# Input checks next to their operands' first readers, and the gate checked through the output's row sums

## The chip, the cores and the metric

The kernel runs on one core of a Trainium2 chip. The time is the device time of one execution in microseconds (us); less is better. The engines of the core are named as the profile names them: PE (TensorE, the matmuls; PEld its weight loads), DVE (VectorE), ACT (ScalarE), POOL (GpSimd) and SP, whose queue issues the DMAs. Each engine works through its own list of instructions in order, and they wait for each other by semaphores.

## The reference

Three blocks follow each other on 4 batches of 768 tokens with 8 heads of 48 (384 features):

```python
for t in range(S):                                   # gated linear attention, state 48x48 for each head
    state = alpha[:, :, t, :, None] * state + einsum('bhd,bhe->bhde', k[:, :, t], v[:, :, t])
    y[:, :, t] = einsum('bhd,bhde->bhe', q[:, :, t], state)
xn = (x - mean) / sqrt(var + 1e-6) * g_ln            # first MLP, x is y with the heads side by side
x = x + maximum(xn @ w_ch1, 0) @ w_ch2               # 384 -> 1536 -> 384
h = gelu(x @ w_in)                                   # second MLP: 384 -> 1024 = u (512) and v (512)
v_n = (v - mean) / sqrt(var + 1e-6) * g_ln2
v_s = einsum('ts,bsd->btd', w_sg, v_n) + b_sg        # mixes all 768 tokens of a batch
out = x + (u * v_s) @ w_out                          # 512 -> 384
```

All inputs and the output are float32. The mixing by `w_sg` needs v_n of a whole batch, so the gate and the output of a batch follow its last chunk.

## The kernel before

**Two halves for each number.** The fast path multiplies in float16: each factor is split into a high half (a copy to float16) and a low half (the rest), and three products (high by high, high by low, low by high) are added in PSUM. The copies to the high half run on ACT, the low halves mostly on DVE or POOL (the helper `low`, L155). This is sound only while the numbers keep within certain windows, so the kernel gathers statistics as it goes: `accum_out` of an instruction writes a sum for each partition into a column of a small table (st_in, st_g, st_xs and others). At the end of the program a chain of small DVE instructions (L1107 to L1114) compares the tables with their bounds and yields one flag. With the flag set a slow float32 path would compute everything anew; in the runs here it stays unset.

**Chunks and units.** 24 chunks of 128 tokens (6 for each batch) pass through attention (`att_steps`), two chunks form a group for the MLP work, and the MLP work is cut into units:

- A (L717): hidden layer of the first MLP, one PSUM tile pg at a time from a ring "g" of three; ACT takes the high half with the ReLU (hT, L722) and DVE the low half (hT, L723). The next A matmuls need a free PSUM tile, and B needs hT.
- B (L752): second matrix of that MLP; DVE adds the residual (L755, with a row sum).
- T: splits x (L151, L152) and transposes it by DMA, and squares x on ACT (L775).
- C (pgv L799, pgu L828): first matrix of the second MLP; ACT applies the GELU (vg L802, uT L831), DVE normalizes v.
- D (pgs L856): the mixing by `w_sg`, once a batch; DVE adds the bias (tm, L862), POOL multiplies by u (L865), ACT copies the high half (L869), the low half follows, and ACT squares the gate tm into a scratch tile for the sum st_g (L872). This last trio is held back in `gate_pending` and issued in order behind later work.
- E (pgo L890): the output product; DVE adds the residual (x, L892), and SP writes the result.

**Attention of a chunk from 6 on.** Decays come as scans over alpha (F and K; L361 from chunk 8 on). For chunks from 8 on q, k and alpha are transposed through a copy on ACT (L298), a DMA transpose on SP (L301) and a joining copy on ACT (L314). F is scaled by q and K by k (L319, `scaled`), F is copied to qs (L446), K to kh (L468), kh is transposed by DMA to ks, K is rescaled on ACT (L482), the scores sc (L490) are masked on DVE (L503) and split into ss (L522 on ACT, low half on DVE). v is split into vs (L549 on ACT, L551 on DVE). The state's update psd (L585) needs vs and ks, the output psy (L621) needs ss and vs. The state is split into sp (L647), y is normalized (L654 to L661) into xsp and goes by DMA to xhT, which A reads.

**The input checks** stand in a step of their own behind the split of v (`stats`): ACT squares q, k and v (L564, three instructions a chunk), DVE takes the largest alpha (L567). The squares' results go to a scratch tile from a ring "cv" of two buffers (`junk`), which the gate squares (L872), the squares of x (L775) and the pieces of w_sg on their way to the DMA transposes (wsp, L221) use too. A buffer of that ring comes free when its last use is done. The raw inputs of a chunk lie in one of two buffers (inp); the next chunk but one is loaded into it by four DMAs on SP when all its readers are done.

**What sets the order.** Every step and unit gets a planned time, all are sorted by it, and the program is written in that order. The framework's scheduler then builds each engine's list from its own estimate of when an instruction can run, so an instruction that is made free earlier can move past others on every engine. `issue_after` and `in_order` hold an instruction behind a named one.

## Time and profile before

| | us |
|---|---|
| median of 3 runs (lowest to highest) | 686.86 (686.51 to 688.11) |
| profiled execution, its own time | 688.59 |
| its span | 686.8 |
| PE busy | 640.7 |
| DVE busy | 442.2 |
| ACT busy | 412.1 |
| POOL busy | 237.3 |

The span is the traced part of the profiled execution; 1.79 us of its own time lie outside. The mean granted TensorE clock of the span is 0.981 of full speed. "L717 PE MATMUL pg<-xhT,w1s" in a row is the kernel's line, the engine, the operation, and the tiles written and read; "[1.67 <-DVE hT L723]" behind a stretch says that the engine stood idle for 1.67 us before it and that DVE's hT of line 723 ended that.

### The profile page before, as it was taken

To read this page: it belongs to the slowest core of one execution; us is meant where nothing else is said; L and a number is where in the kernel's file an instruction comes from. 1 tells how busy PE (TensorE), PEld (TensorE's weight loads), DVE (VectorE), ACT (ScalarE), POOL (GpSimd) and SP (SyncE) were. 2 spreads that over 40 slices of the span, in tenths; PEclk is the share of its full clock that TensorE was granted. 3 is DMA by queue.
4 is the path that set the end of the run, shared out by engine and by line. 5 is a ranking of instruction groups with operands and counts; after the bars stand their busy time and mean duration, and the time that the engine had idled before them with its cause. 6 is when DMAs were issued, how large, how long until landed. Compare 5 with 4: busy or idle time off the path is not lost.

```text
span 686.8 us, 14367 instructions
## 1 busy us (share of the span) xinstructions
PE 640.7 (93%) x5622; PEld 487.2 (71%) x5622; DVE 442.2 (64%) x852; ACT 412.1 (60%) x787; POOL 237.3 (35%) x462
## 2 busy tenths in 40 slices
PE   5989798989999989999999989998989999999995
PEld 3677586667676876677677876676666986676783
DVE  6799977867745576557745569658756686233334
ACT  3765445687873698498773788767663873232230
POOL 4132210533423650443533751532405660301251
PEclk9999979999999998999999999999999999999999
DMA  9996879648363468466263387754263402200102
GB/s 226 279 246 177 259 168 185 105 88 118 64 107 53 72 110 152 105 113 110 48 112 51 60 116 158 123 105 70 51 89 62 86 17 70 24 12 12 35 2 75
DMA packets 228637, 70.64 MB, mean 103 GB/s; under 512 B 219472, under 2 KB 222544, under 8 KB 228560
## 3 DMA queue, kind: packets, MB, share of 16 engines
q1 hardware_dynamic: 228560, 69.63, 53.3%
q8 instruction: 46, 0.75, 0.5%
q14 instruction: 31, 0.25, 0.1%
HBM read 35.79 MB, written 4.72 MB: 59 GB/s over the span
## 4 chain that ended last, share of the span: by engine, by line
PE 51%; DMA 15%; DVE 14%; ACT 11%; issue 4%; POOL 2%; SPq 1%; ACTq 0%; DVEq 0%; POOLq 0%
PE pg L752 12%; PE pg L717 10%; PE pgs L856 9%; PE pgo L890 5%; PE pgu L828 5%; DMA stage<-stage 5%; PE pgv L799 4%; DMA wgs<-wsp 3%; ACT stage L314 2%; DMA stage<-in_moe_w_ch_dram 2%; DMA xhT<-xsp 2%; DMA inp<-in_q_dram 2%; ACT stage L298 2%; PE sc L490 1%; DVE sc L503 1%
## 5 line engine op out<-in xcount | busy, mean ns | idle before, releaser
L717 PE MATMUL pg<-xhT,w1s 128*128 128x256 f16 (+1 forms) x1404 | 152.5, 268 | 10.6 <-DVE hT L723 9.4
L717 PEld LDWEIGHTS <-w1s 128*128 128x128 f16 x1404 | 130.1, 100 | 28.7 <-issue 9.0
L752 PE MATMUL pg<-w2s,hT 128*128 128x384 f16 x864 | 146.6, 328 | 0.4 <-DVE hT L723 0.4
L752 PEld LDWEIGHTS <-hT 128*128 128x128 f16 x864 | 83.8, 98 | 54.3 <-issue 1.4
L856 PE MATMUL pgs<-wgs,vn 128*128 128x256 f16 x864 | 96.0, 273 | 0.0
L856 PEld LDWEIGHTS <-vn 128*128 128x128 f16 x864 | 84.1, 98 | 10.3
L723 DVE SCALAR_TENSOR_TENSOR hT<-pg,hT 128x512 f16<-128x512 f32 (+1 forms) x74 | 49.2, 673 | 44.8 <-ACT hT L722 44.6
L314 ACT ACTIVATE stage<-stage 128x1024 uint16<-128x1024 uint16 x48 | 64.4, 1351 | 16.2 <-DMA stage<-stage 16.2
L298 ACT ACTIVATE stage<-inp 128x1024 uint16<-128x1024 uint16 x48 | 49.8, 1051 | 26.2 <-DVE K L361 8.8
L155 POOL TENSOR_TENSOR kh<-K,kh 128x512 f16<-128x512 f32 x17 | 21.0, 1238 | 102.3 <-ACT kh L468 102.3
L722 ACT ACTIVATE hT<-pg 128x512 f16<-128x512 f32 (+1 forms) x74 | 42.0, 572 | 17.5 <-PE pg L717 17.1
L828 PE MATMUL pgu<-x2T,wis 128*128 128x256 f16 x432 | 49.6, 273 | 1.7 <-ACT vg L802 0.9
L799 PE MATMUL pgv<-wis,x2T 128*128 128x512 f16 x216 | 49.3, 379 | 1.8 <-DVE hT L723 1.8
L890 PE MATMUL pgo<-wos,uT 128*128 128x384 f16 x288 | 48.6, 326 | 0.1
L828 PEld LDWEIGHTS <-wis 128*128 128x128 f16 x432 | 41.8, 98 | 8.3 <-issue 1.8
L155 POOL TENSOR_TENSOR qs<-F,qs 128x512 f16<-128x512 f32 x18 | 20.2, 1121 | 76.8 <-ACT qs L446 76.8
L865 POOL TENSOR_TENSOR tm<-tm,uT 128x512 f32<-128x512 f32 x24 | 32.9, 1372 | 23.6 <-DVE tm L862 23.2
L890 PEld LDWEIGHTS <-uT 128*128 128x128 f16 x288 | 27.7, 98 | 18.0 <-issue 0.3
L862 DVE SCALAR_TENSOR_TENSOR tm<-pgs,g2c,bbc 128x256 f32<-128x256 f32 x48 | 20.9, 477 | 28.9 <-PE pgs L856 17.6
L799 PEld LDWEIGHTS <-x2T 128*128 128x128 f16 x216 | 20.5, 97 | 24.0 <-issue 1.9
L522 ACT ACTIVATE ss<-sc 128x512 f16<-128x512 f32 x36 | 20.8, 591 | 24.0 <-DVE sc L503 23.9
L869 ACT ACTIVATE uT<-tm 128x512 f16<-128x512 f32 x24 | 15.0, 626 | 30.0 <-POOL tm L865 30.0
(184 smaller groups left out, 1094.0 us busy)
## 6 DMA issues: line engine op xcount, KB each, us to landing
stage<-in_moe_w_ch_dram SPq DMA_DIRECT2D x24, 384.0 KB, 5.3
inp<-in_alpha_dram SPq DMA_DIRECT2D x24, 192.0 KB, 3.6
inp<-in_q_dram SPq DMA_DIRECT2D x24, 192.0 KB, 3.4
inp<-in_k_dram SPq DMA_DIRECT2D x24, 192.0 KB, 4.0
inp<-in_v_dram SPq DMA_DIRECT2D x24, 192.0 KB, 4.3
out_dram<-x SPq DMA_DIRECT2D x24, 192.0 KB, 1.9
stage<-in_moe_w_in_dram SPq DMA_DIRECT2D x4, 768.0 KB, 4.8
stage<-in_moe_w_sg_dram SPq DMA_DIRECT2D x6, 384.0 KB, 4.1
```

Of the source, the lines that this page charges most:

```text
L155: (nc.vector if on_dve else nc.gpsimd).tensor_tensor(out=out, in0=in0, in1=in1, op=ALU.subtract)
L298: nc.scalar.activation(out=sp, in_=t[:, n].rearrange("p h d -> p (h d)").bitcast(U16) .rearrange("p (x w) -> p w x", w=2), func=AF.Copy)
L314: nc.scalar.activation(out=words[:, :, :, gap:], in_=tr, func=AF.Copy)
L717: nc.tensor.matmul(out=pg[:, f, :], lhsT=w1s[:, a, kk, ff * P:(ff + 1) * P], rhs=xhT[j][:, r, kk, o], start=(n_ == 0), stop=(n_ == 3 * KD ...
L722: nc.scalar.activation(out=hi, in_=src, func=AF.Relu)
L723: last_dve[0] = nc.vector.scalar_tensor_tensor(out=lo, in0=src, scalar=0.0, in1=hi, op0=ALU.max, op1=ALU.subtract)
L752: nc.tensor.matmul(out=box[s], lhsT=hidden(a, f, s), rhs=w2s[:, r, f, :], start=(f == 0 and a == 0 and r == 0), stop=(f == KF - 1 and r == 1))
L799: nc.tensor.matmul(out=pg, lhsT=x2T[j][:, a, kk, o], rhs=wis[:, r, kk, DG:DI], start=(n_ == 0), stop=(n_ == 3 * KD - 1))
L828: nc.tensor.matmul(out=pg[:, f, :], lhsT=wis[:, a, kk, ff * P:(ff + 1) * P], rhs=x2T[j][:, r, kk, 0:N], start=(n_ == 0), stop=(n_ == 3 * K ...
L856: nc.tensor.matmul(out=pg[:, f, :], lhsT=vn[b * NCH + s][:, a, d * P:(d + 1) * P], rhs=wgs[th][:, r, s, :], start=(n_ == 0), stop=(n_ == 3 ...
L865: nc.gpsimd.tensor_tensor(out=tm, in0=tm, in1=uT[key][:, o, :], op=ALU.mult)
L890: nc.tensor.matmul(out=pg, lhsT=gt[key][:, d // 2, a, d % 2, o], rhs=wos[:, r, d, :], start=(d == 0 and a == 0 and r == 0), stop=(d == KG ...
```

## The change

For the 18 chunks from 6 on, the squares of q and k leave the step behind the split of v. They are issued in the step that takes the low half of kh and starts the transpose to ks, each held behind the first instruction that reads the scaled operand (the copy to qs, the copy to kh). The largest alpha is issued in the same step, held behind the scaling of F. The square of v stays where all three were. In the gate, L872 stays for the last batch only (six of 24), and st_g shrinks to six columns. For batches 0 to 2 the output's residual addition gets an `accum_out`, which writes the row sum of each of the 18 output chunks to a new table st_o; the flag's chain compares it with its bounds in three more DVE instructions.

```diff
-    st_g = big.tile([P, NC], F32, name="st_g")
+    st_g = big.tile([P, 6], F32, name="st_g")
+    st_o = big.tile([P, NC - NCH], F32, name="st_o")
...
-                scaled("F", "q")
+                T["q scaled"] = scaled("F", "q")
...
-                nc.scalar.activation(out=T["qs"][:, 0], in_=T["F"], func=AF.Copy)
+                T["q read"] = nc.scalar.activation(out=T["qs"][:, 0], in_=T["F"], func=AF.Copy)
...
                 low(chosen(HB), T["kh"][:, 1], T["K"], T["kh"][:, 0])
                 if "ks" not in T:
                     work(["ks"], F16)
+
+                for n, first in enumerate((T["q read"], T["k read"][0])):
+                    with tc.issue_after(first.ins):
+                        square(n)
+                with tc.issue_after(T["q scaled"].ins):
+                    nc.vector.tensor_reduce(out=st_in[:, i, 3:4], in_=t[:, 3, :, 0:D], op=ALU.max, axis=AX.XY,
+                                            apply_absolute_value=True)
                 nc.sync.dma_start_transpose(out=T["ks"].rearrange("p a n d -> p (a n) d"),
                                             in_=T["kh"].rearrange("p a n t -> p (a n t)"))
...
+        def square(n):
+            nc.scalar.activation(out=junk()[:, 0:DM].rearrange("p (h d) -> p h d", h=H), in_=t[:, n, :, 0:D],
+                                 func=AF.Square, accum_out=st_in[:, i, n:n + 1])
...
         def stats():
             with tc.issue_after(T["v last"][0].ins):
-                for n in range(3):
-                    nc.scalar.activation(out=junk()[:, 0:DM].rearrange("p (h d) -> p h d", h=H),
-                                         in_=t[:, n, :, 0:D], func=AF.Square, accum_out=st_in[:, i, n:n + 1])
-            with tc.issue_after(T["v last"][1].ins):
-                nc.vector.tensor_reduce(out=st_in[:, i, 3:4], in_=t[:, 3, :, 0:D], op=ALU.max, axis=AX.XY,
-                                        apply_absolute_value=True)
+                square(2)
...
-                        n_ = b * 6 + 2 * th + dp
-                        nc.scalar.activation(out=junk()[:, 0:512].rearrange("p (a b) -> p a b", a=2), in_=tm,
-                                             func=AF.Square, accum_out=st_g[:, n_:n_ + 1])
+                        if b == B - 1:
+                            n_ = 2 * th + dp
+                            nc.scalar.activation(out=junk()[:, 0:512].rearrange("p (a b) -> p a b", a=2), in_=tm,
+                                                 func=AF.Square, accum_out=st_g[:, n_:n_ + 1])
...
                 nc.vector.scalar_tensor_tensor(out=xs[i], in0=pg, scalar=1.0 / (S_G * S_WO), in1=xs[i],
-                                               op0=ALU.mult, op1=ALU.add)
+                                               op0=ALU.mult, op1=ALU.add,
+                                               accum_out=st_o[:, i:i + 1] if b < B - 1 else None)
...
-            (st_g, 0.0, 2.0 ** 31, [NC]),
+            (st_g, 0.0, 2.0 ** 31, [6]),
+            (st_o, -1e30, 1e30, [NC - NCH]),
```

The diff shows little of what moves, since the scheduler sets the lists. Three places follow; in the changed kernel the same instruction has a line number one to twelve higher (L314 is L315, L722 is L729, L522 is L534, the squares are L494, x's square L782).

**ACT, between the gate of batch 0 and its output product.** xsp is the split of an attention output or of x, uT<-tm the high half of the gate, hT the hidden layer's high half, inp_94 and inp_95 (inp_95 and inp_96 in the changed kernel) the two input buffers. Before:

```order
L446 ACTIVATE qs<-F 128x512
L314 ACTIVATE stage<-stage 128x2x512
L647 ACTIVATE sp<-state 128x384
L549 ACTIVATE vs<-inp_95 128x384
L314 ACTIVATE stage<-stage 128x2x512
L660 ACTIVATE xsp<-psy,nmu 128x384
L151 ACTIVATE xsp<-x 128x384
L722 ACTIVATE hT<-pg 128x512
L869 ACTIVATE uT<-tm 128x512
L872 ACTIVATE junk,st_g<-tm 128x512
L775 ACTIVATE junk,st_xm<-x 128x384
L722 ACTIVATE hT<-pg 128x512 x2
```

Now:

```order
L447 ACTIVATE qs<-F 128x512
L494 ACTIVATE junk,st_in<-inp_96 128x384 x2
L654 ACTIVATE sp<-state 128x384
L315 ACTIVATE stage<-stage 128x2x512
L561 ACTIVATE vs<-inp_96 128x384
L667 ACTIVATE xsp<-psy,nmu 128x384
L152 ACTIVATE xsp<-x 128x384
L494 ACTIVATE junk,st_in<-inp_96 128x384
L729 ACTIVATE hT<-pg 128x512
L876 ACTIVATE uT<-tm 128x512
L729 ACTIVATE hT<-pg 128x512 x2
```

The three input squares now stand ahead of the first hT (two of them ahead of sp and vs); the gate square and x's squares no longer stand between the first hT and the next two. A gate square just ahead of qs, above the rows shown, is gone as well. The same holds one batch later.

**DVE at the same place.** Before:

```order
L551 SCALAR_TENSOR_TENSOR vs<-inp_95,vs 128x384
L567 TENSOR_REDUCE st_in<-inp_95 128x1
L661 SCALAR_TENSOR_TENSOR xsp<-psy,st_mv,xsp 128x384
L152 SCALAR_TENSOR_TENSOR xsp<-x,xsp 128x384
L723 SCALAR_TENSOR_TENSOR hT<-pg,hT 128x512
L155 TENSOR_TENSOR uT<-tm,uT 128x512
L503 TENSOR_TENSOR sc<-sc,causal 128x512 x2
L361 SCALAR_TENSOR_TENSOR F<-stage,reset 128x516
L361 SCALAR_TENSOR_TENSOR K<-stage,reset 128x516
L723 SCALAR_TENSOR_TENSOR hT<-pg,hT 128x512 x2
```

Now:

```order
L563 SCALAR_TENSOR_TENSOR vs<-inp_96,vs 128x384
L668 SCALAR_TENSOR_TENSOR xsp<-psy,st_mv,xsp 128x384
L153 SCALAR_TENSOR_TENSOR xsp<-x,xsp 128x384
L730 SCALAR_TENSOR_TENSOR hT<-pg,hT 128x512
L156 TENSOR_TENSOR uT<-tm,uT 128x512
L730 SCALAR_TENSOR_TENSOR hT<-pg,hT 128x512
L515 TENSOR_TENSOR sc<-sc,causal 128x512
L730 SCALAR_TENSOR_TENSOR hT<-pg,hT 128x512
L515 TENSOR_TENSOR sc<-sc,causal 128x512
L362 SCALAR_TENSOR_TENSOR F<-stage,reset 128x516
L362 SCALAR_TENSOR_TENSOR K<-stage,reset 128x516
```

The second and third hT moved from behind both score masks and both scans to ahead of the scans, and the reduction of alpha left this place.

**ACT while the last weights are prepared** (chunk 6; wsp are the pieces of w_sg). Before:

```order
L151 ACTIVATE wsp<-stage 128x768
L722 ACTIVATE hT<-pg 128x512
L134 ACTIVATE bits<-stage 128x768
L151 ACTIVATE wsp<-stage 128x768
...
L549 ACTIVATE vs<-inp_94 128x384
L564 ACTIVATE junk,st_in<-inp_94 128x384 x2
...
L564 ACTIVATE junk,st_in<-inp_94 128x384
L814 ACTIVATE vn<-vg 128x512
L298 ACTIVATE stage<-inp_94 128x1024 x3
L522 ACTIVATE ss_1525<-sc 128x512
L314 ACTIVATE stage<-stage 128x2x4x128
L522 ACTIVATE ss_1526<-sc 128x512
```

Now:

```order
L447 ACTIVATE qs<-F 128x512
L494 ACTIVATE junk,st_in<-inp_95 128x384
L838 ACTIVATE uT<-pgu 128x512
L469 ACTIVATE kh<-K 128x512
L494 ACTIVATE junk,st_in<-inp_95 128x384
L152 ACTIVATE wsp<-stage 128x768
...
L152 ACTIVATE wsp<-stage 128x768
L315 ACTIVATE stage<-stage 128x2x4x128
L315 ACTIVATE stage<-stage 128x2x512
L299 ACTIVATE stage<-inp_95 128x1024
L494 ACTIVATE junk,st_in<-inp_95 128x384
L534 ACTIVATE ss_1531<-sc 128x512
```

The last two pieces of w_sg moved behind the squares of q and k, with which they share the ring "cv", and both ss moved behind the square of v and one more joining copy.

## The prediction, made before the changed kernel was run

> **What bounds the kernel now.** I read the page first, then busy time by stage, then the timeline of TensorE (PE) at every place where it stops, and last the two engines that it waits for there.
>
> ```profile
> span 686.8 us, 14367 instructions
> PE 640.7 (93%) x5622; PEld 487.2 (71%) x5622; DVE 442.2 (64%) x852; ACT 412.1 (60%) x787; POOL 237.3 (35%) x462
> L717 PE MATMUL pg<-xhT,w1s 128*128 128x256 f16 (+1 forms) x1404 | 152.5, 268 | 10.6 <-DVE hT L723 9.4
> L752 PE MATMUL pg<-w2s,hT 128*128 128x384 f16 x864 | 146.6, 328 | 0.4 <-DVE hT L723 0.4
> ...
> 254.00:268.00 14.00, 10.11 (x71) 7.41 (x72) 13.06 (x21) 13.32 (x30) 2.59 (x6) 0.76 0.68 125
> 268.00:400.00 132.00, 132.00 (x1204) 98.67 (x1202) 79.66 (x155) 90.69 (x174) 55.41 (x102) 1.00 0.53 90
> 400.00:420.00 20.00, 16.13 (x163) 13.22 (x160) 14.11 (x28) 19.36 (x41) 8.23 (x13) 0.91 0.76 124
> ```
>
> The last three rows are stretches of the span: their length, then busy time of PE, weight loads, DVE, ACT and POOL, then PE's granted clock, the DMA share and GB/s. PE is busy 640.7 of 686.8 us. From 268 to 400 it is busy 132.00 of 132.00: there work taken off ACT or DVE is worth nothing, and work put on them costs nothing until it makes PE wait. Money lies only where PE stops. I call three such places A (120 to 147, where the last weights are still being prepared), C (254 to 268, between the gate of batch 0 and its output product) and D (400 to 420, the same place of batch 1). At C and D ACT is nearly full (13.32 of 14, 19.36 of 20), and ACT is the engine from which the change takes work. At C the granted clock is 0.76 too, so a stop costs more than its idle time.
>
> ```profile
> 254.91 0.59 PE L585 MATMUL psd<-vs,ks 128*128 128x96 f16 x10 [0.74 <-DVE vs L551]
> 257.17 3.17 PE L717 MATMUL pg<-xhT,w1s 128*128 128x256 f16 x18 [1.67 <-DVE hT L723]
> 261.82 5.59 PE L717 MATMUL pg<-xhT,w1s 128*128 128x256 f16 x36 [1.48 <-DVE hT L723]
> 267.24 4.06 PE L890 MATMUL pgo<-wos,uT 128*128 128x384 f16 x24
> ...
> 411.09 3.48 PE L717 MATMUL pg<-xhT,w1s 128*128 128x256 f16 x18 [1.67 <-DVE hT L723]
> 415.74 4.10 PE L717 MATMUL pg<-xhT,w1s 128*128 128x256 f16 x36 [1.17 <-DVE hT L723]
> ```
>
> Each row is a stretch of matmuls: start, length, form, count, and in brackets the idle time before it and what ended that. At C PE idles 0.74 + 1.67 + 1.48 = 3.89 us, at D 1.67 + 1.17 = 2.84. The 36 matmuls at D took 4.10 us; at C the same 36 took 5.59, 1.49 more, and 18 take 3.17 and 3.48 where half of 4.10 is 2.05: 1.12 and 1.43 lost to a slow clock. Recovering everything would be worth 3.89 + 1.12 + 1.49 = 6.50 at C and 2.84 + 1.43 = 4.27 at D, 10.8 together. That is the most these two places hold. The other 9.4 - 1.67 - 1.48 - 1.67 - 1.17 = 3.4 us that L717 waits for DVE lie where the new order leaves the squares behind the same neighbours as before; I put 0 there.
>
> **The change, part by part.** First the pieces.
>
> ```profile
> L872 ACT ACTIVATE junk<-tm x24: 612/614/625, 233.5 to 670.9; 128x512 bf16<-128x512 f32 x24
> L872 ACT ACTIVATION_READ_ACCUMULATOR junk<-tm x24: 185/187/198, 234.0 to 671.4; 128x1 f32 x24
> L564 ACT ACTIVATE junk<-inp x54: 506/509/527, 129.8 to 568.3; 128x384 bf16<-128x384 f32 x54
> L567 DVE TENSOR_REDUCE st_in<-inp x18: 514/540/548, 131.3 to 565.9; 128x1 f32<-128x384 f32 x18
> L892 DVE SCALAR_TENSOR_TENSOR x<-pgo,x x24: 547/557/558, 269.4 to 679.6; 128x384 f32<-128x384 f32 x24
> L755 DVE SCALAR_TENSOR_TENSOR x<-pg,rx,x x24: 595/612/619, 83.1 to 632.7; 128x384 f32<-128x384 f32 x24
> L755 DVE DVE_READ_ACCUMULATOR x<-pg,rx,x x24: 76/84/89, 83.6 to 633.2; 128x1 f32 x24
> 679.65 0.56 DVE L892 SCALAR_TENSOR_TENSOR x<-pgo,x 128x384 f32<-128x384 f32 x1 [1.34 <-PE pgo L890]
> ```
>
> *Gate squares removed*: 18 of 24. One is 0.614 us and its accumulator read 0.187, which overlaps it by about 0.1, so a step of 0.70; 18 make 12.6 us of ACT. Six fall in each of batches 0 to 2; in each, four run before C's or D's stretch while PE is full, one just ahead of qs there and one between two of the hT evictions. In batch 2 nothing waits for them. So 4 of the 12.6 us lie beside a stop at most: one square (0.70) ahead of the first hT at C and one behind it, and the same at D.
>
> *Row sums of the output*: L892 gains an accumulator. The row of L755 is the same operation with one: 0.612 against 0.557 and 0.084 for the read, so 0.055 + 0.084 = 0.14 each, 18 times 2.5 us of DVE. They lie beside 24 output matmuls of 4.06 us (two outputs, 2.03 each, against 0.56 + 0.14). I take 0; 2.5 with the cover gone, and 0 below. *One more verdict* (three DVE operations of about 0.17 by the neighbouring rows of the tail) ends beside the 1.34 us in which DVE waits for the last output: 0, else 0.5.
>
> *Squares of q and k moved*: 36 of L564's 54, each 0.509 + about 0.1, so 0.6. ACT does as much in all, but each now stands behind its operand's first reading. At C the two put 1.2 us ahead of sp and vs; v's square now stands ahead of the first hT too.
>
> ```profile
> 251.62 1.34 ACT L314 ACTIVATE stage<-stage 128x1024 uint16<-128x1024 uint16 x1
> 253.23 0.51 ACT L549 ACTIVATE vs<-inp 128x384 f16<-128x384 f32 x1
> 255.71 0.58 ACT L722 ACTIVATE hT<-pg 128x512 f16<-128x512 f32 x1
> 257.83 1.06 ACT L722 ACTIVATE hT<-pg 128x512 f16<-128x512 f32 x2
> ...
> 256.43 0.69 DVE L723 SCALAR_TENSOR_TENSOR hT<-pg,hT 128x512 f16<-128x512 f32 x1
> 257.63 1.29 DVE L503 TENSOR_TENSOR sc<-sc,causal 128x512 f32<-128x512 f32 x2
> 261.09 1.26 DVE L723 SCALAR_TENSOR_TENSOR hT<-pg,hT 128x512 f16<-128x512 f32 x2
> ```
>
> *Place C.* Ahead of the first hT on ACT (255.71) one gate square goes (-0.70) and three input squares come (+1.8): the first hT is 1.1 late, the 18 matmuls start at 257.17 + 1.1 = 258.3, and the vs wait grows by as much inside that same stretch. Queued behind those squares are L314, vs, xsp and hT; PE waits for the last. Then it turns. Before, DVE's second hT waited from 258.9 (ACT had it) to 261.09, behind two score masks (1.29) and two scans. Now two of the evictions stand ahead of the scans, so the second wait (1.48) ends before PE comes to it. 258.3 + 3.17 (the slow figure) + 4.10 to 5.59 (the fast and the slow 36) is 265.6 to 267.1. The output product also needs the fourth hT's read of its PSUM buffer, which I place near 265.8. Against 267.24 that is -1.6 to -0.1; I take -1.1, nearer to the fast row since one wait less precedes. Bounds: -6.5 if everything recovers, +2 if all three squares land in front (+1.8) and nothing is regained.
>
> *Place D.* The same ACT and DVE order. 411.09 + 1.1 + 3.48 + 4.10 = 419.8 against 415.74 + 4.10 = 419.84: 0; with the 18 at full clock -1.4. Between: -0.5.
>
> *Place A.* The timeline of PE there, and the transposes of w_sg that matter for it:
>
> ```profile
> 124.93 2.13 PE L828 MATMUL pgu<-x2T,wis 128*128 128x256 f16 x18 [0.80 <-DVE nmu L658]
> 139.95 0.20 PE L621 MATMUL psy<-vs,ss 128*128 128x48 f16 x1 [1.37 <-ACT ss L522]
> 142.17 0.22 PE L621 MATMUL psy<-vs,ss 128*128 128x48 f16 x1 [1.00 <-ACT ss L522]
> 146.96 1.26 PE L717 MATMUL pg<-xhT,w1s 128*128 128x256 f16 x10
> ...
> L221 SPq DMA_TRANSPOSE wgs<-wsp x12: 1211/1244/2502, 87.2 to 123.3; - x12
> DMA to landing us min/median/max: 2.7/3.6/5.9
> ```
>
> PE idles 0.80 + 1.37 + 1.00 = 3.17 us here. The squares write the scratch ring of two buffers that the last w_sg pieces (wsp) use too, and a buffer comes free when SP's transpose of it (L221) has landed. In the new ACT order both wsp pieces stand behind the squares of q and k instead of ahead of them. That takes two DVE operations away from ahead of nmu (the 0.80 goes), and it puts 16 more L752 matmuls (146.6 / 864 = 0.17 each, 2.7 us) ahead of the first psy: PE, which is there at 139.95 - 1.37 = 138.6 now, comes at 138.6 - 0.8 + 2.7 = 140.5. But v's square now waits for the last of those transposes, and both ss stand behind v's square and a second L314 (1.34): I place the first psy at 142.5, 2.6 later than now. PE waits once for about 2, and what remains (7 L752, 1.2 us, and 24 psy, with the second ss half a microsecond behind the first) takes some 3: L717 starts at about 145.4, with an episode of slow clock at 146.5, against 146.96. I take -1.0. Bounds: -3.2 (no wait left) and +3: two transposes in a row at 5.9 instead of 3.6, 2 x 2.3 = 4.6, less the 1.6 by which 145.4 lies ahead.
>
> The Trainium skill bears on this, in TensorE: Matmul & The Clock Gate, "Why this matters for your kernels": it asks that no idle gap between matmul bursts pass about 3 us, or the clock drops. No gap at C or D passes 1.67, yet 18 matmuls took 3.17 us there: the trace does not agree. By the page those 18 would run in 2.05, C would come to the PSUM bound of 265.8 (-1.4 in place of -1.1), and a wait at A that passes 3 us would be the only dangerous one, which speaks against the change.
>
> *A new wait in batch 1.* One chunk's score matmuls move there from the stage of the gate inputs into the next unit, and the first two vg reads of PSUM then stand on ACT behind L314, K and, for the second, two squares.
>
> ```profile
> 475.06 0.78 PE L490 MATMUL sc<-F,K 48*128 48x128 f32 x8 [1.52 <-ACT K L482]
> 479.42 2.13 PE L828 MATMUL pgu<-x2T,wis 128*128 128x256 f16 x18 [0.86 <-ACT vg L802]
> ```
>
> Nothing in batch 1 waits like that before; these two rows of a later chunk show the same arrangement at 1.52 + 0.86 = 2.4. PE has other matmuls queued there, so I take +0.7 between 0 and 2.4.
>
> *Abs-max of alpha*, 18 x 0.54 on DVE, moved behind the scaling of F: no row waits for it; it lets alpha's buffer go earlier, and so SP's next alpha load: 0, at most 0.54 once.
>
> **Sum**: -1.1 - 0.5 - 1.0 + 0.7 + 0 = -1.9. The profiled execution took 688.59 us, 1.79 outside its span of 686.8; it would take 686.7. The median of the runs is 686.86, 1.73 below that execution, so 685.0.
>
> **Rivals.** *Full recovery* (faster): ACT's 0.70s and the earlier hT close C and D altogether and the clock stays up: 10.8, so 676.1; at three quarters of it 678.8. For: ACT is full there and loses work. Against: the first hT comes later, not sooner.
>
> *The squares delay what PE waits for* (slower): ACT takes its queue in order, so squares that used to stand behind the evictions now stand ahead of vs and hT at C and D (+1.8 each, +2 with the lost regain at one of them), and at A the ring of two makes v's square wait for a w_sg transpose. It decides once the last transpose lands more than 1.6 us after its median. Price: 1.8 + 0.7 = 2.5 at least and 3 + 2 + 1.3 = 6.3 at most, so 689.4 to 693.2, with its middle near 690.5 since the dear end needs all at once. For: in all three places the new order of ACT has squares nearer to the front. Against: at C and D DVE's turn gives back 1.48 and 1.17.
>
> *Nothing moves on PE's path* (same): what is late before a wait is caught up by the next: 686.9. For: D comes out at 0 by one of its two readings, and 268 to 400 hides everything.
>
> **Chances.** Small net gain 0.42 (own range 683 to 687), full recovery 0.15, delay 0.28, nothing 0.15. About 0.2%, 1.4 us, is what a measurement of this kernel tells from no change: the bounds are 685.5 and 688.2. Of the 0.42, 0.31 lie below the lower bound, 0.08 between, 0.03 above; of the 0.28, 0.03 between. Faster 0.31 + 0.15 = 0.46, same 0.08 + 0.03 + 0.15 = 0.26, slower 0.03 + 0.25 = 0.28. For 8 times in 10 the range reaches from a little beyond three quarters of the full recovery, 678, to 691 in the delay.
>
> **What would show it.** ACT should lose 18 L872 and be busy some 12.6 us less; L892 should be 0.14 longer in 18 of 24. At C and D the second wait of L717 should be gone and the first longer; the first pgo row should start about a microsecond earlier by PE's own work. At A one long psy wait of about 2 us should stand in place of the waits of 0.80, 1.37 and 1.00. I am wrong if C or D still shows two hT waits, if A's psy wait passes 4 us with v's square idle on a wgs transpose ahead of it, or if batch 1 shows a stop over 2.4.

## The result, and the profile after

The changed kernel takes 683.02 us (median of 5 runs, 682.0 to 684.42) against 686.51 us (5 runs, 685.55 to 688.11): a ratio of 0.9945, with a 95% interval of 0.9921 to 0.9968. That is 3.5 us less; the forecast was 685.0 after 686.86, 1.9 less. The profiled executions differ more, 682.0 against 688.59, because the one of before was 2.1 us above its median and the other 1.0 below. The page of the changed kernel begins so, with the same three stretches behind it:

```profile
span 680.2 us, 14363 instructions
PE 640.2 (94%) x5622; PEld 487.7 (72%) x5622; DVE 441.2 (65%) x873; ACT 400.0 (59%) x751; POOL 234.5 (34%) x462
...
254.00:268.00 14.00, 12.38 (x90) 9.02 (x89) 12.55 (x24) 10.73 (x19) 1.37 (x3) 0.88 0.63 100
268.00:400.00 132.00, 131.04 (x1211) 98.15 (x1209) 79.64 (x160) 89.14 (x170) 54.01 (x102) 1.00 0.53 93
400.00:420.00 20.00, 17.28 (x145) 13.68 (x143) 13.81 (x27) 16.58 (x33) 6.85 (x13) 0.91 0.59 107
```

PE has the same work (640.2 us against 640.7), ACT 12.1 less, in 36 instructions fewer (18 squares and 18 accumulator reads). In the 14 us of C PE is busy 12.38 instead of 10.11 us and ACT 10.73 instead of 13.32. The timeline of PE in the changed kernel, at C and D, then A, then the place near 475, and batch 1:

```profile
253.87 0.58 PE L592 MATMUL psd<-vs,ks 128*128 128x96 f16 x10 [0.35 <-DVE vs L563]
255.87 7.72 PE L724 MATMUL pg<-xhT,w1s 128*128 128x256 f16 x54 [1.41 <-DVE hT L730]
263.44 2.11 PE L898 MATMUL pgo<-wos,uT 128*128 128x384 f16 x12
265.77 6.50 PE L898 MATMUL pgo<-wos,uT 128*128 128x384 f16 x39 [0.21 <-DVE hT L730]
...
406.93 0.24 PE L592 MATMUL psd<-vs,ks 128*128 128x96 f16 x2 [0.75 <-ACT vs L561]
407.52 0.59 PE L592 MATMUL psd<-vs,ks 128*128 128x96 f16 x10 [0.35 <-DVE vs L563]
409.51 7.72 PE L724 MATMUL pg<-xhT,w1s 128*128 128x256 f16 x54 [1.41 <-DVE hT L730]
417.08 2.11 PE L898 MATMUL pgo<-wos,uT 128*128 128x384 f16 x12
419.41 4.06 PE L898 MATMUL pgo<-wos,uT 128*128 128x384 f16 x24 [0.21 <-DVE hT L730]
...
142.20 0.20 PE L628 MATMUL psy<-vs,ss 128*128 128x48 f16 x1 [0.72 <-ACT ss L534]
144.15 0.68 PE L628 MATMUL psy<-vs,ss 128*128 128x48 f16 x20 [0.49 <-DVE ss L156]
144.67 2.13 PE L724 MATMUL pg<-xhT,w1s 128*128 128x256 f16 x18
...
470.86 0.71 PE L502 MATMUL sc<-F,K 48*128 48x128 f32 x8
474.31 2.12 PE L835 MATMUL pgu<-x2T,wis 128*128 128x256 f16 x18
...
320.83 2.12 PE L835 MATMUL pgu<-x2T,wis 128*128 128x256 f16 x18 [0.31 <-ACT vg L809]
323.70 2.60 PE L759 MATMUL pg<-w2s,hT 128*128 128x384 f16 x15 [0.33 <-ACT vg L809]
```

At C and D the second wait for hT is gone, and the 18 and 36 matmuls have become one stretch of 54. It takes 7.72 us where 54 at D's full rate (4.10 for 36) would take 6.15, so 1.6 us of slow clock remain. At A two waits, 0.72 and 0.49, stand in place of the three. Near 475, where PE idled 1.52 and 0.86 us, it does not idle now. In batch 1 three small waits are new (0.32 at 306.23 beside the two shown).

### The profile page after: what moved, and what is told of

Read it like the earlier page. It is cut to its first block, busy times and chain, and to the rows that moved or that the text cites. A ratio compares the mean times of both kernels' runs of the same rounds, so it can differ in the third digit from the quotient of the medians.

```text
span 680.2 us, 14363 instructions
## 1 busy us (share of the span) xinstructions
PE 640.2 (94%) x5622; PEld 487.7 (72%) x5622; DVE 441.2 (65%) x873; ACT 400.0 (59%) x751; POOL 234.5 (34%) x462
## 4 chain that ended last, share of the span: by engine, by line
PE 49%; DVE 20%; ACT 14%; DMA 10%; issue 3%; POOL 2%; SPq 1%; ACTq 0%; DVEq 0%; POOLq 0%
PE pg L759 12%; PE pgs L863 8%; PE pg L724 7%; PE pgo L898 6%; PE pgv L806 5%; PE pgu L835 4%; ACT stage L315 3%; DVE hT L730 2%; DMA stage<-stage 2%; DVE K L362 2%; DVE F L362 2%; DVE sc L515 2%; DMA wgs<-wsp 2%; ACT junk L494 2%; DVE ss L156 2%
## 5 line engine op out<-in xcount | busy, mean ns | idle before, releaser
L724 PE MATMUL pg<-xhT,w1s 128*128 128x256 f16 (+1 forms) x1404 | 153.3, 269 | 8.2 <-DVE hT L730 7.2
L724 PEld LDWEIGHTS <-w1s 128*128 128x128 f16 x1404 | 130.9, 100 | 26.0 <-issue 9.2
L759 PE MATMUL pg<-w2s,hT 128*128 128x384 f16 x864 | 144.6, 326 | 0.8 <-DVE hT L730 0.4
L759 PEld LDWEIGHTS <-hT 128*128 128x128 f16 x864 | 83.8, 98 | 54.4 <-issue 0.9
L315 ACT ACTIVATE stage<-stage 128x1024 uint16<-128x1024 uint16 x48 | 64.6, 1354 | 19.2 <-DMA stage<-stage 19.0
L729 ACT ACTIVATE hT<-pg 128x512 f16<-128x512 f32 (+1 forms) x74 | 42.0, 574 | 25.4 <-PE pg L724 25.3
L872 POOL TENSOR_TENSOR tm<-tm,uT 128x512 f32<-128x512 f32 x24 | 31.9, 1333 | 29.5 <-DVE tm L869 29.4
L247 POOL TENSOR_SCALAR ve<-mvv 128x1 f32<-128x1 f32 x24 | 5.9, 244 | 79.9 <-DVE mvv L813 78.9
```

Source lines behind the costliest of these rows:

```text
L315: nc.scalar.activation(out=words[:, :, :, gap:], in_=tr, func=AF.Copy)
L724: nc.tensor.matmul(out=pg[:, f, :], lhsT=w1s[:, a, kk, ff * P:(ff + 1) * P], rhs=xhT[j][:, r, kk, o], start=(n_ == 0), stop=(n_ == 3 * KD ...
L729: nc.scalar.activation(out=hi, in_=src, func=AF.Relu)
L759: nc.tensor.matmul(out=box[s], lhsT=hidden(a, f, s), rhs=w2s[:, r, f, :], start=(f == 0 and a == 0 and r == 0), stop=(f == KF - 1 and r == 1))
L872: nc.gpsimd.tensor_tensor(out=tm, in0=tm, in1=uT[key][:, o, :], op=ALU.mult)
```

## The experiments

Twelve kernels ran, four to a chip, each beside runs of the kernel before. Two of them are the program of before, once as it is and once with its tiles shifted, and they came out at 1.0010 (0.9990 to 1.0029) and 1.0024 (1.0003 to 1.0044): differences of less than about 0.3% between two of these kernels mean nothing.

**The gate part alone** (its diff is that of the change on st_g, st_o, L872, L892 and the table of checks):

```diff
+                        if b == B - 1:
+                            n_ = 2 * th + dp
                             nc.scalar.activation(... func=AF.Square, accum_out=st_g[:, n_:n_ + 1])
...
-                                               op0=ALU.mult, op1=ALU.add)
+                                               op0=ALU.mult, op1=ALU.add,
+                                               accum_out=st_o[:, i:i + 1] if b < B - 1 else None)
```

> The gate part alone: 18 gate squares gone, row sums of the output instead; all three input squares and the largest alpha stay behind the split of v. The traces of before and after put the change's gain at A (-1.0 to -1.3 us), C (-2.4) and near 475 (-1.9), with D about 0. My theory: C's gain comes from the gate, because without its squares ACT enters C earlier (kh 1.4 us earlier in the changed kernel) and DVE does the second and third hT ahead of the scans. Then this kernel has C's 2.4 us, no gain at A (the pieces of w_sg stand ahead of the squares as before: four waits of 0.80, 0.63, 1.37, 1.00), and lies at -2 to -3 us, 684. The rival (C's gain comes from the squares' new place): no more than 0.7 at C, and 686.

Measured: 1.0011 (0.9988 to 1.0035). PE at C in this kernel:

```profile
255.29 0.24 PE L586 MATMUL psd<-vs,ks 128*128 128x96 f16 x2 [0.88 <-ACT vs L550]
256.29 0.46 PE L586 MATMUL psd<-vs,ks 128*128 128x96 f16 x7 [0.75 <-DVE vs L552]
258.49 4.00 PE L718 MATMUL pg<-xhT,w1s 128*128 128x256 f16 x18 [1.75 <-DVE hT L724]
262.37 4.97 PE L718 MATMUL pg<-xhT,w1s 128*128 128x256 f16 x36
...
325.48 2.12 PE L829 MATMUL pgu<-x2T,wis 128*128 128x256 f16 x18 [0.87 <-ACT vg L803]
```

The sum of the theory, -2 to -3 us, falls. DVE takes two hT ahead of the scans here too, and the 1.48 is gone, but vs comes later (0.88 + 0.75 instead of 0.74), so that the first 18 start at 258.49 instead of 257.17 (0.9 us later, as this profile was 0.4 late before C), and batch 1 has a new wait of 0.87. Some 11 us less busy time on ACT (401.1 against 412.1) won nothing in all; where it wins and loses is told at the last kernel below.

**The input checks alone** (the change without its gate part):

```diff
+                for n, first in enumerate((T["q read"], T["k read"][0])):
+                    with tc.issue_after(first.ins):
+                        square(n)
+                with tc.issue_after(T["q scaled"].ins):
+                    nc.vector.tensor_reduce(out=st_in[:, i, 3:4], ...)
```

> The input checks alone: squares of q and k and the largest alpha moved, all 24 gate squares kept and no row sums. My theory: A as in the changed kernel (-1.0 to -1.3 us, the wait for nmu gone, one psy wait), C less than half of 2.4 because ACT still does the gate squares there although DVE's second and third hT stand ahead of the scans, and the stop near 475 gone if it hangs on when the inputs are loaded (-1.9): -2 to -4 us in all, 683 to 684.5. The rival (the gate squares are what matters): within 1 us of before.

Measured: 0.9961 (0.9942 to 0.9981), 2.7 us by the 687.14 of before beside it. The rival falls. Three rows of PE:

```profile
142.40 0.22 PE L627 MATMUL psy<-vs,ss 128*128 128x48 f16 x1 [3.95 <-ACT ss L533]
142.44 1.45 PE L758 MATMUL pg<-w2s,hT 128*128 128x384 f16 x4
...
264.42 2.86 PE L896 MATMUL pgo<-wos,uT 128*128 128x384 f16 x15 [2.66 <-DVE hT L729]
```

A has its single wait. At C the earlier hT and the full clock bring PE to pgo so early that it waits 2.66 us for the fourth hT; pgo still starts 2.8 us before the 267.24 of the first profile. The stop near 475 is absent.

**Only alpha's largest value moved:**

```diff
-            with tc.issue_after(T["v last"][1].ins):          # in stats()
-                nc.vector.tensor_reduce(out=st_in[:, i, 3:4], ...)
+                with tc.issue_after(T["q scaled"].ins):       # beside the transpose to ks
+                    nc.vector.tensor_reduce(out=st_in[:, i, 3:4], ...)
```

> Only the largest alpha is moved behind the scaling of F; squares of q, k and v, and the gate, as before. DVE's second and third hT stay behind both scans at C here. My theory: no gain at A and none at C (its waits 0.74, 1.67 and 1.48 stay within 0.3), so 0 to -0.5 us; if the stop near 475 (1.52 + 0.86) is due to when alpha's load goes out, it goes here: -2. The rival, that taking 0.54 us of DVE from behind vs starts hT earlier: -0.5 at each of C and D.

Measured: 0.9962 (0.9943 to 0.9982), and the -2 came by the second of the three ways: no stop near 475, none near 505 either. At C its waits did not stay:

```profile
256.47 2.12 PE L720 MATMUL pg<-xhT,w1s 128*128 128x256 f16 x18 [1.45 <-DVE hT L726]
261.11 4.11 PE L720 MATMUL pg<-xhT,w1s 128*128 128x256 f16 x36 [2.52 <-DVE hT L726]
266.48 1.78 PE L893 MATMUL pgo<-wos,uT 128*128 128x384 f16 x10 [1.27 <-DVE hT L726]
```

The wait behind the scans is 2.52 here and pgo waits 1.27 more: with DVE's order left as it was, one instruction less ahead of hT only moves the idle time. By PE's progress, as it is cut in the next section, this kernel loses 2.1 us in batch 1 and 1.3 at D against the first profile of before, and wins 2.3 from 438 to 499 and 2.8 from 499 to 531, where the stops near 475 and 505 stood: its gain lies there.

**Only the squares of q and k moved:**

```diff
             with tc.issue_after(T["v last"][0].ins):          # in stats()
-                for n in range(3): square(n)
+                square(2)                                     # q and k: beside the transpose to ks
```

> Only the squares of q and k are moved; the largest alpha and the gate stay. DVE's order at C is that of the changed kernel (two hT ahead of the scans), ACT's is that of before with the gate squares. My theory: A's gain is here (-1.0 to -1.3 us: the wsp pieces stand behind the squares), C between 0 and -1.5 by DVE's turn alone, so -1 to -3 us in all. The rival, that the change's gain at A needs alpha's reduction moved as well: A as before and -1 at most.

Measured: 0.9941 (0.9916 to 0.9967), 4.1 us by the same 687.14: as much as the whole change, and more than expected. The rival falls; A's gain is here, though this profile also enters A 1.4 us late and so has that much to catch up:

```profile
140.80 0.20 PE L627 MATMUL psy<-vs,ss 128*128 128x48 f16 x1 [1.67 <-ACT ss L530]
```

**Before, once more:**

> The kernel before, unchanged, as a second profile and a second set of times: what two executions of one program differ by, stage by stage. The ratio should be 1.000 within 0.002. If the stop near 475 (1.52 + 0.86 us) and its DMA transpose of 4.8 us show again, they belong to this program and not to chance; if not, a gain of 2 us there in other kernels' single profiles proves nothing.

The ratio is given above. PE at C and near 475 in this profile of the unchanged program:

```profile
257.41 3.69 PE L717 MATMUL pg<-xhT,w1s 128*128 128x256 f16 x18 [1.67 <-DVE hT L723]
262.06 4.11 PE L717 MATMUL pg<-xhT,w1s 128*128 128x256 f16 x36 [0.96 <-DVE hT L723]
266.88 4.06 PE L890 MATMUL pgo<-wos,uT 128*128 128x384 f16 x24 [0.72 <-DVE hT L723]
...
477.83 1.36 PE L828 MATMUL pgu<-x2T,wis 128*128 128x256 f16 x11 [0.41 <-ACT vg L802]
```

Two readings of the first profile were one execution's. The 36 matmuls at C run at full clock here (4.11, not 5.59), and yet pgo starts only 0.4 us earlier, since it then waits 0.72 for the fourth hT: most of that slow clock had cost nothing. And the stop near 475 is 0.41 in place of 2.38, as the transposes it hung on landed in time.

**The gate part without row sums** (the check of the gate of batches 0 to 2 is left out):

```diff
                                                op0=ALU.mult, op1=ALU.add)   # no accum_out, no st_o
```

> The gate part without its row sums: 18 gate squares gone and nothing in their place (the check of the gate of batches 0 to 2 is left out). If the row sums on DVE cost what the removal wins, this is faster than the gate part alone by 1 us or more, and the prediction's 0 for them was wrong. My theory: nothing on PE's path waits for them, so it lies within 0.5 us of the gate part alone, at the time of before.

Measured: 0.9920 (0.9894 to 0.9947), some 6 us faster than before and than the gate part with row sums. But of the 8.6 us by which this profile's last output comes earlier than before's, 4.4 are there at 212 us, where no gate and no output has run, and up to where both kernels have the same lists of instructions. Its loads land sooner from the start. The DMA row of the first MLP's weights here, and in the gate part alone with row sums and the tiles where they lay before (below):

```profile
stage<-in_moe_w_ch_dram SPq DMA_DIRECT2D x24, 384.0 KB, 4.6
```

```profile
stage<-in_moe_w_ch_dram SPq DMA_DIRECT2D x24, 384.0 KB, 5.3
```

So this run does not price the row sums; something else differs. Without st_o all tiles allocated behind it lie 96 bytes lower than in the gate part and 64 lower than before. The last four kernels tested that.

**Before without any square of q, k and v** (their check is left out):

```diff
             with tc.issue_after(T["v last"][0].ins):
-                for n in range(3): nc.scalar.activation(... func=AF.Square, accum_out=st_in[:, i, n:n + 1])
+                pass
...
-        nc.vector.memset(st_in[:, 0:NF, :], 1.0)
+        nc.vector.memset(st_in, 1.0)
```

> The kernel before without any square of q, k and v (54 instructions, 33 us of ACT; the check of the inputs' size is left out). It bounds what the place of the squares can be worth: if the change wins because squares leave ACT's crowded stretches at A, C and D, this wins at least as much, -4 to -6 us in all. If it wins no more than 2 us, the gain of the moved squares lies in the order of something else that moved with them (the loads, the w_sg pieces).

Measured: 0.9919 (0.9894 to 0.9944), 5.6 us: the squares in their old place cost that, and moving two thirds of them won 4.1. The total is the theory's, the places are only in part. Against the first profile of before, by PE's progress, A is 1.0 us shorter and D 1.3; C is 3.3 shorter and batch 1 3.2 longer, so that they cancel; and 2.3 and 2.2 us are won from 438 to 497 and from 497 to 531, which the theory did not name.

**The whole change, alpha's largest value left in place:**

```diff
-                with tc.issue_after(T["q scaled"].ins):
-                    nc.vector.tensor_reduce(out=st_in[:, i, 3:4], ...)      # back to stats()
```

> The whole change but with alpha's largest value left where it was: squares of q and k moved, gate checked by row sums. The squares alone gave a ratio of 0.994 and the whole change 0.9945. If the parts add up with the gate at 0, this gives 0.994 too, and alpha's move adds nothing to the squares' (against alpha alone, which gave 0.996); if alpha's move is needed, it is at 0.998.

Measured: 1.0001 (0.9982 to 1.0020). Neither answer held: the squares without the gate part gave 0.9941, and the gate part took all of it back. PE at C, and the stop near 475:

```profile
253.19 0.24 PE L592 MATMUL psd<-vs,ks 128*128 128x96 f16 x2 [1.03 <-ACT vs L558]
254.18 0.58 PE L592 MATMUL psd<-vs,ks 128*128 128x96 f16 x10 [0.74 <-DVE vs L560]
...
472.45 0.78 PE L499 MATMUL sc<-F,K 48*128 48x128 f32 x8 [1.62 <-ACT K L487]
```

With the gate squares gone the list of ACT puts both input squares ahead of sp and vs at C; with the gate squares there (the kernel of the squares alone) all three of the chunk's squares stand behind the third hT. That costs little at C itself: pgo starts at 263.81 here and at 263.54 with the squares alone. Of the 4.6 us by which this profile ends later than that one, 2.3 lie from 438 to 497, where this one has the stop (1.62 + 0.86) and the other 0.37; 0.8 lie in batch 1, 0.7 at D and 0.4 at C. The parts do not add up, and each builds another list; that the lists alone are the reason is not shown, since the stop near 475 also comes and goes with one and the same list.

**Before, the tiles shifted by 64 bytes:**

```diff
-    st_g = big.tile([P, NC], F32, name="st_g")
+    st_g = big.tile([P, NC + 16], F32, name="st_g")[:, 0:NC]
```

> The kernel before with one table 64 bytes longer, so that every tile allocated after it lies 64 bytes further on; each engine's list of instructions is the same. The gate part without row sums was 0.992 and differed from the gate part (1.001) long before the first gate, with loads that landed 0.4 to 0.9 us sooner: its tiles lie 96 bytes lower than with the row sums. Theory: the place of the tiles in SBUF modulo 128 bytes sets how long DMAs take; here the stage tiles lie at 0 modulo 128 as there (64 in the kernel before), so this is faster by 5 to 6 us, 681, and the weight loads land in 4.6 us instead of 5.3. Rival: the row sums cost that time; then this stays at 1.000 within 0.002.

Measured: 1.0024 (1.0003 to 1.0044). The weight loads land in 5.2 us. The theory of the place modulo 128 bytes falls.

**The changed kernel, its two tables in one** of 160 bytes, and then of 96 bytes:

```diff
-    st_g = big.tile([P, 6], F32, name="st_g")
-    st_o = big.tile([P, NC - NCH], F32, name="st_o")
+    st_go = big.tile([P, 40], F32, name="st_g")       # 24 instead of 40 in the second
+    st_g, st_o = st_go[:, 0:6], st_go[:, 6:24]
```

> The changed kernel with its two tables in one of 160 bytes, so that the tiles behind them lie as in the last kernel (stage at 0 modulo 128 bytes instead of 96). Same lists of instructions as the changed kernel. Theory (the place of the tiles): 5 us or more faster than the changed kernel, ratio 0.985 to 0.988 against before. Rival (row sums cost): 0.9945 as the changed kernel.

> The changed kernel with its two tables in one of 96 bytes, so that every tile lies where it lay before; the changed kernel had moved them by 32 bytes. Same lists of instructions. If the shift of 32 bytes helped the change, this is slower than 0.9945 (0.998 if that was most of its gain); if it did nothing, 0.9945; if it hurt, as the gate part's 1.001 against 0.992 suggests, faster: 0.990.

Measured: 0.9961 (0.9944 to 0.9979) and 0.9950 (0.9933 to 0.9967). Both are the changed kernel's 0.9945 within their intervals: the 32 bytes by which the change shifts the tiles play no part, and the gain is that of the instructions.

**The gate part alone, tiles where they lay before:** the same one table of 96 bytes.

> The gate part alone with its tables in the 96 bytes of before: nothing but the instructions differs from before. It measures what 18 gate squares less on ACT and 18 row sums more on DVE are worth without the shift: 0.9965 to 0.999 by the prediction's reasons (some of C's stop), 1.001 again if the shift of 32 bytes plays no part.

Measured: 1.0026 (1.0007 to 1.0044), no different from the copy of before on that chip (1.0024). The gate part alone is worth nothing that can be measured. It does win at C (from 247 to 303 this kernel is 1.7 us shorter than the mean of three profiles of before's lists, the first gate kernel 0.5), but both are 1.3 us longer in batch 1. What makes the kernel without row sums faster stays open: its lists up to the first output are those of this kernel, a shift by +64 and one by +32 bytes did nothing, and a shift by -64 with the row sums in was not run.

## Why the prediction was right or wrong, point by point

The sign, the case (a small net gain) and the range were right; the time was forecast 1.9 us lower and came 3.5 lower. That it came so near is in part luck: by the table below C was missed by 1.4 us and batch 1 by 1.8, in opposite directions.

For the stages, PE is followed in six profiles: three of before's lists (the first profile, the copy, the shifted copy) and three of the changed kernel's. All run the same 5622 matmuls, the two lists in different orders. A stretch is cut only where all six have started the same matmuls, so nothing but waits, the clock and the cost of going from one kind of matmul to another can make it longer. The cuts bear the time of the first profile. (An instruction of DVE will not do as a cut: the 14th x of L755, at 374.64 in the first profile, has 18 matmuls of L856, 2.0 us of work, less ahead of it in the changed lists.) The last x of L892 starts at 679.65 in the first profile of before and 5.7 us earlier in the changed kernel:

```profile
673.94 0.56 DVE L900 SCALAR_TENSOR_TENSOR x<-pgo,x 128x384 f32<-128x384 f32 x1 [0.64 <-PE pgo L898]
```

How much longer (+) or shorter each stretch is than in the first profile of before, in us, and the difference of the means (the first profile counts as 0 in that of before) beside the forecast:

| stretch | before: copy, shifted | changed: own, 160 bytes, 96 bytes | means differ by | forecast |
|---|---|---|---|---|
| 83 to 161 (A) | -0.4, -0.3 | -2.2, -1.7, -0.9 | -1.4 | -1.0 |
| 161 to 247 | +0.6, +0.6 | +1.3, +0.7, +0.8 | +0.5 | 0 |
| 247 to 303 (C) | -0.7, -0.7 | -3.1, -2.9, -2.9 | -2.5 | -1.1 |
| 303 to 401 (batch 1) | 0.0, 0.0 | +2.5, +2.5, +2.5 | +2.5 | +0.7 |
| 401 to 438 (D) | +0.9, +0.7 | -1.3, -1.1, -1.2 | -1.7 | -0.5 |
| 438 to 497 | -2.1, +0.1 | -2.3, -2.4, -2.5 | -1.7 | 0 |
| 497 to 531 | 0.0, +0.2 | -0.7, -0.7, -0.6 | -0.7 | 0 |
| 531 to 677 | 0.0, 0.0 | +0.1, +0.1, +0.1 | +0.1 | 0 |

The means sum to -4.9, more than the medians' 3.5; one stretch of one program differs by up to 2 us between two profiles (438 to 497).

**Place A: the order was right, what ACT waits for was not.** Forecast were the first psy at 142.5 and L717 at 145.4, with the wait for nmu gone. Measured are 142.20 and 144.67, no wait for nmu, and in the two other profiles of the changed lists psy comes at 141.2 and 142.1. How long PE waits there depends on when it arrives (0.72, 3.36, 3.26 us, forecast about 2); when psy comes is set by ACT. The forecast episode of slow clock came in those two, not in the first. Rows of ACT and PE in the last of them:

```profile
137.60 2.54 ACT L315 ACTIVATE stage<-stage 128x1024 uint16<-128x1024 uint16 x2 [4.03 <-DMA stage<-stage]
142.08 0.20 PE L628 MATMUL psy<-vs,ss 128*128 128x48 f16 x1 [3.26 <-ACT ss L534]
144.84 3.31 PE L724 MATMUL pg<-xhT,w1s 128*128 128x256 f16 x18
```

The experiments point to the squares without separating them cleanly. From 83 to 161 the kernels with the squares of q and k moved are shorter than the first profile of before (-4.1 squares alone and -4.1 with the gate, which enter 1.4 and 1.1 us late; -0.6 checks alone); of those without, alpha alone is +0.5, the gate alone -0.3 and -1.4, no squares at all -1.0, and the one without row sums, in which all loads were faster, -3.6. So the checks alone lie among those without. The prediction had v's square, and so ss behind it, wait for the transpose of a w_sg piece. That wait is 0.20 us in the changed kernel's first profile and absent in the other two; the rival's price there was not paid. What ACT stands idle for is the transpose that the two joining copies (L315) need, which stand ahead of that square and of ss: 2.25, 3.74 and 4.03 us in the three, and 4.20 with the checks alone.

**Place C: right in kind, the size was off by one false start.** "the first hT is 1.1 late" failed. The prediction held the time fixed at which ACT reaches the place, and counted only what comes and goes there. But the squares of the preceding chunk stood right ahead of kh in the list of before, behind two gate squares (at 239.04 and 240.35), and all of these had left too. ACT before, and then in the changed kernel:

```profile
241.44 0.51 ACT L564 ACTIVATE junk<-inp 128x384 bf16<-128x384 f32 x1
242.42 0.52 ACT L564 ACTIVATE junk<-inp 128x384 bf16<-128x384 f32 x1
243.91 0.51 ACT L564 ACTIVATE junk<-inp 128x384 bf16<-128x384 f32 x1
244.41 0.61 ACT L468 ACTIVATE kh<-K 128x512 f16<-128x512 f32 x1
```

```profile
242.99 0.63 ACT L469 ACTIVATE kh<-K 128x512 f16<-128x512 f32 x1 [0.79 <-DVE K L320]
250.08 0.52 ACT L494 ACTIVATE junk<-inp 128x384 bf16<-128x384 f32 x1
254.50 0.59 ACT L729 ACTIVATE hT<-pg 128x512 f16<-128x512 f32 x1
```

kh starts 1.4 us earlier, 0.6 of it beyond what PE has won by then (0.84 at 212), and is now held by DVE, no longer by ACT. So the first hT comes at 254.50, 1.2 us earlier instead of 1.1 later. The rest of the step held: DVE's second and third hT run ahead of the scans, the second wait (1.48) is gone, and the fourth hT bounds pgo (0.21 here, 2.66 in the checks alone), at 263.44 for pgo's first half and 265.77 for its second. The steps priced for ACT were a little long: the gate square at 256.71 in the first profile holds the queue for 0.61 us, not 0.70, and an input square for 0.51 (250.08 to 250.59 in the changed one), not 0.6. And the gate part by itself came to nothing in all.

**Place D: the same step failed.** -1.7 against -0.5, since the same late first hT was assumed. The prediction also left a stop of before out of its 2.84 us there:

```profile
408.84 0.59 PE L585 MATMUL psd<-vs,ks 128*128 128x96 f16 x10 [0.88 <-DVE vs L551]
```

With it PE stopped for 0.88 + 1.67 + 1.17 = 3.72 us at D, and 10.8 as the most that C and D hold should have read 11.7. In the changed kernel it stops for 0.75 + 0.35 + 1.41 + 0.21 = 2.72. The 54 matmuls still lose to the slow clock (7.72), as 18 of them did before (3.48); that was half written off, and nothing came of it.

**Batch 1: the wait was priced, the pieces were not.** +2.5 against +0.7. Three waits make 0.96 of it (0.32 + 0.31 + 0.33). The rest does not show as idle time. The score matmuls (sc), which run 16 in a row in before, stand in pieces of 2, 4 and 12 between others now:

```profile
367.46 1.16 PE L490 MATMUL sc<-F,K 48*128 48x128 f32 x16
368.56 4.07 PE L752 MATMUL pg<-w2s,hT 128*128 128x384 f16 x24
```

```profile
341.38 0.49 PE L502 MATMUL sc<-F,K 48*128 48x128 f32 x4
341.81 2.14 PE L724 MATMUL pg<-xhT,w1s 128*128 128x256 f16 x18
```

Counted to the start of the next kind, the 16 take 1.10 us (first rows, before) and a piece of 4 takes 0.43 (second rows, changed), not a quarter of 1.10. The 64 from 303 to 401 take 5.5 us in place of 4.6, and the other kinds of matmul there 0.6 more. So what C won, batch 1 took back, and the rival's "268 to 400 hides everything" was not so.

**Not forecast: the place near 475.** I used its rows only as the price of a wait elsewhere and put 0 for it. From 438 to 497 the means differ by 1.7. No stop stands there in the kernels with alpha's largest value moved (five profiles); without the squares one of 0.20 does, with only the squares moved one of 0.37, and in the seven other profiles with alpha in place 2.17 to 2.89 us (K and vg together) in six and 0.41 in the copy of before. So it goes with alpha's move, but an execution without it can escape it. The wait of ACT behind it is for a DMA transpose that takes 4.8 us to land in the first profile, 3.1 in the copy and 3.0 to 3.5 in the changed one; why it was late no run shows. The next two stops, near 505, shrink from 1.36 + 1.79 to 0.82 + 1.61. **Nor from 161 to 247**, where I had said that the new order leaves things as they were: a wait of 0.81 for hT is new at 188.60, and the stretch costs 0.5, about what A had won over its forecast.

**What was costed at nothing stayed so.** Row sums: the two forms of L900 in the changed kernel are

```profile
L900 DVE SCALAR_TENSOR_TENSOR x<-pgo,x x24: 540/558/559, 266.2 to 673.9; 128x384 f32<-128x384 f32 x24
L900 DVE DVE_READ_ACCUMULATOR x<-pgo,x x18: 76/82/84, 266.7 to 631.3; 128x1 f32 x18
```

0.08 each, not 0.14, and PE waits for none of them. From 633 us to the last output no time changed by as much as 0.1 us, the one more verdict included.

**The chances.** The delay had 0.28. Its first half showed in the kernel with all but alpha's move (vs 1.03 + 0.74 late), but C was no slower for it: pgo came at 263.81, against 267.24 in before. What brought that kernel back to 1.0001 lies more near 475 than at C. The full change has waits of 0.35 and 1.41 at C. Full recovery, 0.15, was priced on a slow clock of which, at C, most cost nothing.

**The clock.** The Trainium skill (TensorE: Matmul & The Clock Gate, "Why this matters for your kernels") puts the harm at gaps beyond about 3 us. Three profiles agree. Behind 3.95 us of idle PE in the checks alone, 4 matmuls of L758 took 1.45 us, 0.36 each where 0.17 is usual. Behind 3.26 us at A (rows above) the next 4 of L759 still took 0.81, but the 18 of L724 that follow took 3.31 where 2.13 is usual, at a granted clock of 0.50 from 144 to 147; behind 3.36 us in the other profile they took 3.43. But shorter gaps stand ahead of a slow clock too: behind 1.67 to 1.75 us, with another stop of 0.6 to 1.6 us shortly ahead, the 18 matmuls at C took 3.17, 3.69 and 4.00 us in the first profile, the copy and the gate part, where 2.12 is usual. There the measurement decides. The gaps alone do not settle it, though: behind 0.74 and 1.75 us at D in the gate part with its tiles in place the 18 took 2.12, and behind 1.45 and 2.52 us at C with alpha's move alone 2.12, and 4.11 for the 36. What else decides is open.

## What to carry to other kernels

When work leaves an in-order queue, start the walk before the first place that it leaves: a chunk's moved instructions are missing from the next chunk's stretch too, and that sets when it begins. Where a scheduler builds the lists, the parts of a change need not add up (0.9941 and 1.0011 alone, 1.0001 together): try each alone and the whole, and read the new list at the few places where the bottleneck stops. Before a stop in one profile is priced, look at it in a second profile of the same program: one of 2.4 us here was 0.4 in the next. Compare stages at points where the engine that bounds the kernel has done the same work, and do not take its busy time for progress: in batch 1 it lost 1.5 us while it counted as busy.

## What was not expected of the hardware

A kernel whose lists differ only by 18 row sums and their check was 1% faster (0.9920 against 1.0026), with its weight loads landing in 4.6 instead of 5.3 us and those of v in 3.6 instead of 4.6 from the first stage on, before any row sum runs. Shifting all tiles by 32 or 64 bytes up left the weight loads at 5.0 to 5.3 us and the kernel's time as it was; the cause is not settled. And 11 to 12 us of ACT work removed from an engine that is 97% busy beside PE's stops (19.36 of 20 us at D) was worth nothing alone, while the same engine's squares, moved and not removed, were worth 0.6%.
